# The last product of a fused scan, GLU and ReLU-squared kernel, turned so that the weights stand in the array and 512 tokens move

## The chip, the cores and the metric

One Trainium2 chip, one core of it. The metric is the device time of one execution in microseconds, the median of several runs; lower is better.

## The reference

Three stages follow each other on 3072 tokens of 256 features. The first is a chunked state-space scan over 4 batches and 8 heads, the second a gated feed-forward layer, the third a feed-forward layer with a squared ReLU. Only the third is touched:

```python
def _moe_ref(x, w_gate, w_val, w_out):
    g = x @ w_gate
    silu = g * (1.0 / (1.0 + np.exp(-g)))
    val = x @ w_val
    return (silu * val @ w_out).astype(np.float32)

def _moe2_ref(x, w_in, w_out):          # 256 -> 2048 -> 256
    h = x @ w_in
    r = np.maximum(h, 0.0)
    g = r * r
    return (g @ w_out).astype(np.float32)

def reference(**kwargs):
    attn_out = _attn_ref(**attn_kwargs)          # (4, 8, 768, 32)
    B, H, S, D = attn_out.shape
    x = np.ascontiguousarray(attn_out.transpose(0, 2, 1, 3)).reshape(B * S, H * D)
    x = _moe_ref(x=x, **moe_kwargs)
    return _moe2_ref(x=x, **moe2_kwargs)
```

The output is 3072 rows (tokens) of 256 float32 values, so a row is 1024 bytes.

## The kernel before, in words

**Precision.** A float32 product is made of three products of a reduced float32 type (`F32R`): every operand is split into a high and a low part, and high·high, high·low and low·high are summed in PSUM. So a product of 128 by 128 weights costs three matmuls where plain arithmetic would take one.

**Stages.** The scan works in chunks of 112 tokens, the GLU (`glu`, lines 713 to 827) and the third stage (`relu2`, lines 853 to 934) in tiles of 512 tokens. Activations lie in SBUF with features on partitions and tokens along the row (`xh_all`, `xl_all`: the high and low parts). Their products therefore hold weights in the array and move tokens, and give features on partitions again. The weights arrive by DMA, are converted, and are split into high and low parts (class `Unit`).

**The third stage.** `relu2(i, f, ...)` is called for six token tiles `i` and sixteen blocks `f` of 128 hidden features, 96 calls. Each adds these operations to a graph:

- `front` (line 860, on TensorE): six matmuls that move 512 tokens, 128 hidden features by 512 tokens, into a PSUM bank `h`.
- `relu` (ScalarE, line 870), `square` (VectorE, 873), `high` (ScalarE, 876) and `rest` (VectorE, 880): the squared ReLU, and its split into `p`, high and low.
- `back` (line 882, on TensorE): the last product. Before, tokens stand in the array (128 of `p` at a time, four quarters `q`) and 256 columns of `w_out` move: 4 × 3 = 12 matmuls of 256 columns. They add to two PSUM banks `acc`, each with 2 × 128 tokens on partitions and all 256 output features along the row.
- After the sixteenth `f` the two banks are copied out, one by ScalarE (line 921) and one by VectorE (line 923), and each goes to DRAM in one DMA of 256 KB, whole rows of 1024 bytes (line 927). The sixth tile does this in halves.

**What sets the order.** Every operation has an engine, an estimated cost, a priority, and the buffers it takes from pools: eight PSUM banks (`ps`), four SBUF tiles for `t` and for the copied-out sums `o` (`tmp`), three for `p`. `Graph.order` (lines 50 to 124) replays this graph with the estimated costs and writes out the order in which each engine gets its instructions. A buffer goes to the next operation that asks for its pool, so an operation may wait for whoever used the buffer last: a `relu` that gets a `tmp` tile from which a store reads has to wait for the store to land.

In what follows F20 is the `front` of the 21st call, B20 its `back`; the calls are counted through, from 0 to 95, so that B15 is the last back of the first tile.

Of the kernel before, what the change touches and what calls it, by code (L numbers as in the profile page):

```python
# [8 lines left out]
F32 = mybir.dt.float32  # L9
# [118 lines left out]
def kernel(  # L128
# [13 lines left out]
    nc = tc.nc  # L142
    NB, H, S, D = x.shape
    NS = B.shape[-1]
    T = NB * S
# [5 lines left out]
    NF, NF2 = FF // 128, FF2 // 128  # L151
    P = 128
# [4 lines left out]
    TN = 512  # L157
# [3 lines left out]
    for b in range(NB):  # L161
        t = 0
# [24 lines left out]
    g = Graph(pools)  # L187
# [21 lines left out]
    def new(buf, shape, dtype, tag=None):  # L209
        n = 1  # L210
        for d in shape[1:]:
            n *= d
        if buf.pool in ("L", "ab") and n < 1024:

            t = tp[buf.pool].tile([P, 1024], dtype, tag=buf.pool, name=tag or buf.pool)[:, :n]
            buf.t = t.rearrange("p (a b) -> p a b", a=shape[1]) if len(shape) == 3 else t
        else:
            buf.t = tp[buf.pool].tile(shape, dtype, tag=buf.pool, name=tag or buf.pool)
        if buf.pool == "ps" and fills:


            t = buf.t.rearrange("p a b -> p (a b)") if len(shape) == 3 else buf.t
            t = t[:, : min(n, 256)]
            for _ in range(fills.pop()):
                nc.tensor.matmul(t, idle[:, : shape[0]], idle[:, : t.shape[-1]], start=True, stop=True)  # L225
        return buf.t
# [95 lines left out]
    def dma(eng, n, cost, move, fn, deps=(), prio=0.0, bufs=()):  # L322

        i = g.add(eng, n * cost, fn, deps, prio, bufs, lat=0)
        o = g.add("DMA", move, None, [i], prio, bufs, lat=1700)
        o.issue = i
        return o
# [371 lines left out]
    def product(ps, terms):  # L699
        for i, (l, r) in enumerate(terms):  # L700
            nc.tensor.matmul(ps, l, r, start=(i == 0), stop=(i == len(terms) - 1))  # L701

    acc, seen, fronts, backs = {}, {}, {}, {}
# [7 lines left out]
    GATE, GATE_A = PLAN["gate"]  # L711
# [141 lines left out]
    def relu2(i, f, prio, deps):  # L853
        t0 = i * TN
        d = slice(t0, t0 + TN)
        u = W2[f // 2]
        ph, tb, pb = Buf("ps"), Buf("tmp"), Buf("p")
        late = True

        def front():  # L860
            h = new(ph, [P, TN], F32, "h")
            terms = []
            for k in range(2):
                c = k * 256 + f % 2 * 128
                hi, lo = u.hi.t[:, c : c + 128], u.lo.t[:, c : c + 128]
                terms += [(hi, xh_all[:, k, d]), (hi, xl_all[:, k, d]), (lo, xh_all[:, k, d])]
            product(h, terms)

        def relu():
            nc.scalar.activation(new(tb, [P, TN], F32, "t"), ph.t, AF.Relu)  # L870

        def square():
            nc.vector.tensor_tensor(tb.t, tb.t, tb.t, op=ALU.mult)  # L873

        def high():
            nc.scalar.activation(new(pb, [P, 2, TN], F32R, "p")[:, 0, :], tb.t, AF.Copy)  # L876

        def rest():
            e = nc.vector if late else nc.gpsimd
            e.tensor_tensor(pb.t[:, 1, :], tb.t, pb.t[:, 0, :].bitcast(F32), op=ALU.subtract)  # L880

        def back():
            if f == 0:
                acc[-1 - i] = [new(b, [P, 512], F32, "acc") for b in accbuf[-1 - i]]
            for q in range(4):
                ps = acc[-1 - i][q // 2][:, q % 2 * 256 : q % 2 * 256 + 256]
                tk = slice(q * 128, q * 128 + 128)
                c = 512 + f % 2 * 256
                hi, lo = u.hi.t[:, c : c + 256], u.lo.t[:, c : c + 256]
                for s, (l, r) in enumerate([(0, hi), (0, lo), (1, hi)]):  # L890

                    nc.tensor.matmul(  # L892
                        ps, pb.t[:, l, tk], r,
                        start=(f == 0 and s == 0 and q % 2 == 0), stop=(f == NF2 - 1 and s == 2),
                        skip_group_check=True,
                    )

        if f == 0:
            accbuf[-1 - i] = [Buf("ps") for _ in range(2)]
        ab = accbuf[-1 - i]  # L900

        o1 = g.add("PE", 6 * 232, front, [u.parts, *deps], prio - 10 * PLAN["lead"], [ph, u.hi, u.lo], lat=260)
        o1.keep = lambda: 0 if ab[0].taken else 2
        o = g.add("ACT", 600, relu, [o1], prio - GATE_A, [ph, tb])
        o = g.add("DVE", 690, square, [o], prio - GATE, [tb], port=True)
        o = g.add("ACT", 625, high, [o], prio - GATE_A, [tb, pb])
        o = g.add("DVE", 690, rest, [o], prio - GATE, [tb, pb], port=True)
        bk = g.add("PE", 12 * 120, back, [o], prio, [*ab, pb, u.hi, u.lo], lat=260)
        if f == NF2 - 1:

            cuts = 2 if i == T // TN - 1 else 1
            for m in range(2):
                for c in range(cuts):
                    ob = Buf("tmp")
                    by_act = (m if cuts == 1 else c) == 0
                    w = 512 // cuts

                    def drain(m=m, ob=ob, by_act=by_act, cs=slice(c * w, c * w + w)):
                        ov = new(ob, [P, 512], F32, "o")[:, : w]
                        if by_act:  # L920
                            nc.scalar.activation(ov, acc[-1 - i][m][:, cs], AF.Copy)
                        else:
                            nc.vector.tensor_copy(ov, acc[-1 - i][m][:, cs])

                    def store(ob=ob, by_act=by_act, r0=t0 + m * 256 + c * (w // 2)):
                        q = nc.scalar if by_act and cuts == 2 else nc.sync
                        q.dma_start(
                            out=out[r0 : r0 + w // 2, :].rearrange("(i p) f -> p i f", p=P),
                            in_=ob.t[:, :w].rearrange("p (i f) -> p i f", f=256),
                        )  # L930

                    o = g.add("ACT" if by_act else "DVE", 690 // cuts, drain, [bk], prio - GATE, [ab[m], ob])
                    dma("ACT" if by_act and cuts == 2 else "SP", 1, 480, 700, store, [o], prio, [ob])
        return o1, bk


# [18 lines left out]
    for i, (j, c0, c1, exact) in enumerate(PLAN["cells"]):  # L955
        ti, o = (0, c0 * Q) if c0 < 3 else (1, c0 * Q - cut)
        n = min(c1 * Q, S) - c0 * Q
        for f in (2 * j, 2 * j + 1):
            deps = [ck[k].xf if exact else ck[k].x for k in range(c0, c1)]
# [14 lines left out]
    for s, (tl, f) in enumerate(steps):  # L974
# [8 lines left out]
        deps = fronts[tiles[0]][-1:] + fronts[tiles[1]][-1:] if s == 0 else [step_ops[-1]]  # L983
# [21 lines left out]
    for i in range(T // TN):  # L1005
        deps0 = [o for tl in tiles for o in done_tile[tl] if tl[0] < (i + 1) * TN and tl[1] > i * TN]
        for f in range(NF2):
            prev, _ = relu2(i, f, 30000 + (i * NF2 + f) * 10, [prev, *(deps0 if f == 0 else [])])
# [4 lines left out]
    with tc.manual_schedule():  # L1013
# [13 lines left out]
PLAN = dict(  # L1027
    chunk_at=[3.6, 14.8, 21.8, 0.0, 3.2, 18.0, 18.5],
    unit_at=[4.1, 0, 22.6, 19.4, 20.4, 41.5, 34.2, 27.1, 30.0],
    split_at=[-0.1, -21.6, 22.5, -12.5, -9.6, 27.7, -0.1, -18.9, -33.9],  # L1030
    cells=[
        (5, 3, 7, 0),
        (4, 0, 3, 0),
        (5, 0, 3, 1),
        (3, 3, 7, 1),
# [16 lines left out]
    lead=2.5,  # L1052
# [33 lines left out]
```

## Time and profile before

| what | value |
|---|---|
| median of 3 runs | 663.46 us (663.18 to 665.47) |
| span of the profiled execution | 662.5 us |
| its own time beside the span | not listed apart from the three runs; their median is 1.0 us above the span |
| TensorE busy | 654.8 us, 99% of the span |
| VectorE, ScalarE, GpSimd busy | 415.5, 329.3, 221.9 us |
| granted TensorE clock, mean | 0.999 |
| third stage, first back to last matmul | 396 to 658.5 us |

The busy time of TensorE counts a matmul until its modelled end, so matmuls that follow each other overlap in the table; how fast they follow is read from the chain of work that ended last, which gives the start and the length of every run of equal matmuls. Its start times lie some 0.17 us behind those of the timeline; lengths are the same.

### The profile page before, as it was taken

The numbers are of one execution on the slowest core, as the hardware profiler recorded it, in microseconds if no ns is written. First come the engines' busy times: TensorE is split into PE (matmuls) and PEld (weight loads), VectorE is DVE, ScalarE is ACT, GpSimd is POOL, SyncE is SP. The second block draws the span as 40 slices with busy tenths as digits, with TensorE's granted clock in tenths as the row PEclk, the third lists the DMA queues.
The fourth block names the chain that finished last, engine by engine and source line by source line (L and its number), as shares of the span: only waits on it lengthen the run. The fifth ranks groups of instructions, "written<-read, shape, count | busy, mean of one in ns | idle before, by whom it ended". The sixth has DMA issues, their size and how long they took to land.

```text
span 662.5 us, 10931 instructions
## 1 busy us (share of the span) xinstructions
PE 654.8 (99%) x4297; PEld 560.9 (85%) x4297; DVE 415.5 (63%) x578; ACT 329.3 (50%) x634; POOL 221.9 (34%) x207
## 2 busy tenths in 40 slices
PE   9999999999999999999999999999999999999997
PEld 7888677899877777777788889999999999999996
DVE  7898796667565756677455698454455544544553
ACT  4667444455544444555544584444444444444443
POOL 4005864947555656656564541000000000000000
PEclk9999999999999999999999999999999999999999
DMA  7767447476465456752422220000000100000000
GB/s 176 210 129 153 134 84 145 88 134 123 100 126 94 81 108 113 171 129 50 142 64 63 64 65 0 1 33 1 1 33 0 33 1 1 33 1 0 33 1 33
DMA packets 134819, 48.88 MB, mean 74 GB/s; under 512 B 120304, under 2 KB 123376, under 8 KB 134768
## 3 DMA queue, kind: packets, MB, share of 16 engines
q1 hardware_dynamic: 134480, 47.92, 32.7%
q8 instruction: 34, 0.56, 0.4%
q10 hardware_dynamic: 288, 0.26, 0.1%
q14 instruction: 17, 0.14, 0.1%
HBM read 33.94 MB, written 3.22 MB: 56 GB/s over the span
## 4 chain that ended last, share of the span: by engine, by line
PE 97%; DMA 1%; SPq 0%; ACT 0%; issue 0%; DVE 0%; ACTq 0%
PE acc L892 21%; PE h L701 20%; PE g L701 18%; PE acc L819 16%; PE v L701 13%; PE ys L648 2%; PE ab L552 1%; PE cb L619 1%; DMA raw<-in_moe_w_val_dram 1%; PE ab L225 1%; PE cb L610 1%; PE turn L687 1%; PE g L225 1%; PE cb L225 0%; PE trb L225 0%
## 5 line engine op out<-in xcount | busy, mean ns | idle before, releaser
L892 PE MATMUL acc<-hi,p 128*128 128x256 f32 x768 | 152.1, 282 | 0.0
L892 PEld LDWEIGHTS acc<-hi,p 128*128 128x128 f32 x768 | 125.5, 191 | 3.9
L792 POOL TENSOR_TENSOR p<-t,p 128x512 fp32r<-128x512 f32 (+4 forms) x74 | 98.0, 1326 | 91.4 <-ACT p L787 89.3
L873 DVE TENSOR_TENSOR t<-t 128x512 f32<-128x512 f32 x96 | 69.2, 722 | 66.1 <-ACT t L870 66.0
L892 PE MATMUL acc<-lo,p 128*128 128x256 f32 x384 | 108.6, 283 | 0.0
L880 DVE TENSOR_TENSOR p<-t,p 128x512 fp32r<-128x512 f32 x96 | 67.8, 709 | 57.2 <-ACT p L876 57.2
L870 ACT ACTIVATE t<-h 128x512 f32<-128x512 f32 x96 | 57.5, 599 | 78.6 <-PE h L701 78.3
L768 DVE SCALAR_TENSOR_TENSOR t<-t,g 128x512 f32<-128x512 f32 (+6 forms) x92 | 51.9, 565 | 71.1 <-ACT t L765 71.0
L876 ACT ACTIVATE p<-t 128x512 fp32r<-128x512 f32 x96 | 60.5, 632 | 63.4 <-DVE t L873 59.9
L819 PE MATMUL acc<-p,hi 128*128 128x512 f32 (+4 forms) x296 | 85.7, 372 | 0.0
L892 PEld LDWEIGHTS acc<-lo,p 128*128 128x128 f32 x384 | 73.3, 191 | 3.5
L701 PE MATMUL h<-xh_all,hi 128*128 128x512 f32 x192 | 75.8, 395 | 0.0
L701 PE MATMUL h<-xl_all,hi 128*128 128x512 f32 x192 | 75.8, 395 | 0.0
L701 PE MATMUL h<-xh_all,lo 128*128 128x512 f32 x192 | 74.7, 389 | 0.0
L787 ACT ACTIVATE p<-t 128x512 fp32r<-128x512 f32 (+4 forms) x74 | 42.2, 571 | 62.5 <-DVE t L771 58.9
L765 ACT ACTIVATE t<-g 128x512 f32<-128x512 f32 (+6 forms) x92 | 46.1, 503 | 45.3 <-PE g L701 42.6
L701 PE MATMUL g<-xh_all,hi 128*128 128x512 f32 (+4 forms) x176 | 64.4, 366 | 0.0
L701 PE MATMUL g<-xh_all,lo 128*128 128x512 f32 (+4 forms) x176 | 61.4, 349 | 0.0
L701 PE MATMUL g<-xl_all,hi 128*128 128x512 f32 (+4 forms) x176 | 61.3, 349 | 0.0
L819 PEld LDWEIGHTS acc<-p,hi 128*128 128x128 f32 x296 | 52.1, 188 | 10.3 <-issue 2.9
L771 DVE SCALAR_TENSOR_TENSOR t<-t,v 128x512 f32<-128x512 f32 (+2 forms) x66 | 42.9, 649 | 21.6 <-PE v L701 17.2
L415 POOL TENSOR_TENSOR lo<-v,hi 128x1024 fp32r<-128x1024 f32 x17 | 42.8, 2535 | 32.2 <-ACT hi L410 32.0
(97 smaller groups left out, 1148.6 us busy)
## 6 DMA issues: line engine op xcount, KB each, us to landing
ab<-decay SPq DMA_DIRECT2D x21, 452.0 KB, 4.3
raw<-in_moe_w_out_dram SPq DMA_DIRECT2D x14, 512.0 KB, 5.1
raw<-in_moe_w_in_dram SPq DMA_DIRECT2D x8, 512.0 KB, 4.0
raw<-in_moe_w_gate_dram SPq DMA_DIRECT2D x6, 512.0 KB, 4.0
raw<-in_moe_w_val_dram SPq DMA_DIRECT2D x6, 512.0 KB, 5.1
xa<-in_x_dram SPq DMA_DIRECT2D x24, 112.0 KB, 4.1
out_dram<-o SPq DMA_DIRECT2D x10, 256.0 KB, 2.2
bc<-in_B_dram SPq DMA_DIRECT2D x18, 56.0 KB, 2.5
```

The source lines that it names most:

```text
L415: e.tensor_tensor(self.lo.t, self.v.t, self.hi.t.bitcast(F32), op=ALU.subtract)
L701: nc.tensor.matmul(ps, l, r, start=(i == 0), stop=(i == len(terms) - 1))
L765: nc.scalar.activation(t[:, :n], gg(), AF.Tanh, scale=0.5)
L768: nc.vector.scalar_tensor_tensor(tb.t[:, :n], tb.t[:, :n], 1.0, gg(), op0=ALU.add, op1=ALU.mult)
L771: nc.vector.scalar_tensor_tensor(tb.t[:, :n], tb.t[:, :n], 0.5, vv(), op0=ALU.mult, op1=ALU.mult)
L792: e.tensor_tensor(p[:, 1, :n], tb.t[:, :n], p[:, 0, :n].bitcast(F32), op=ALU.subtract)
L819: nc.tensor.matmul(ps, l, r, start=bank not in done_f, stop=f == NF - 1, skip_group_check=True,)
L870: nc.scalar.activation(new(tb, [P, TN], F32, "t"), ph.t, AF.Relu)
L873: nc.vector.tensor_tensor(tb.t, tb.t, tb.t, op=ALU.mult)
L876: nc.scalar.activation(new(pb, [P, 2, TN], F32R, "p")[:, 0, :], tb.t, AF.Copy)
L880: e.tensor_tensor(pb.t[:, 1, :], tb.t, pb.t[:, 0, :].bitcast(F32), op=ALU.subtract)
L892: nc.tensor.matmul(ps, pb.t[:, l, tk], r, start=(f == 0 and s == 0 and q % 2 == 0), stop=(f == NF2 - 1 and s == 2), skip_group_check=True,)
```

## The change

In the first five of the six token tiles `back` is turned. For each of the two halves `m` of the output features, 128 by 128 weights stand in the array and `p` moves, 512 tokens at once: 2 × 3 = 6 matmuls of 512 columns. `acc` then holds output features on partitions and tokens along the row, which is the wrong way round for the output. So VectorE copies both banks out with `transpose`, which turns every 32 by 32 block within itself: partition 32q + t of the result holds, for each of the 16 groups j of 32 tokens, the 32 features from m·128 + 32q on of token 32j + t. Each half is stored with four DMAs of 64 KB, one for each q, in pieces of 32 features, 128 bytes. The sixth tile is as before. The planner's estimate for a front is lowered from 6 × 232 to 6 × 227 ns, and a turned back is estimated at the same.

```diff
+        turned = i < T // TN - 1
...
         def back():
             if f == 0:
                 acc[-1 - i] = [new(b, [P, 512], F32, "acc") for b in accbuf[-1 - i]]
+            c = 512 + f % 2 * 256
+            if turned:
+                for m in range(2):
+                    w = slice(c + m * 128, c + m * 128 + 128)
+                    for s, (l, r) in enumerate([(u.hi, 0), (u.hi, 1), (u.lo, 0)]):
+                        nc.tensor.matmul(
+                            acc[-1 - i][m], l.t[:, w], pb.t[:, r, :],
+                            start=(f == 0 and s == 0), stop=(f == NF2 - 1 and s == 2),
+                        )
+                return
...
-        o1 = g.add("PE", 6 * 232, front, [u.parts, *deps], prio - 10 * PLAN["lead"], [ph, u.hi, u.lo], lat=260)
+        o1 = g.add("PE", 6 * 227, front, [u.parts, *deps], prio - 10 * PLAN["lead"], [ph, u.hi, u.lo], lat=260)
...
-        bk = g.add("PE", 12 * 120, back, [o], prio, [*ab, pb, u.hi, u.lo], lat=260)
+        bk = g.add("PE", 6 * 227 if turned else 12 * 120, back, [o], prio, [*ab, pb, u.hi, u.lo], lat=260)
         if f == NF2 - 1:
 
-            cuts = 2 if i == T // TN - 1 else 1
+            if turned:
+                for m in range(2):
+                    ob = Buf("tmp")
+
+                    def flip(m=m, ob=ob):
+                        nc.vector.transpose(new(ob, [P, 512], F32, "o"), acc[-1 - i][m])
+
+                    def put(m=m, ob=ob):
+                        for q in range(4):
+                            nc.sync.dma_start(
+                                out=out[t0 : t0 + TN, m * 128 + q * 32 : m * 128 + q * 32 + 32].rearrange(
+                                    "(j t) f -> t j f", t=32
+                                ),
+                                in_=ob.t[q * 32 : q * 32 + 32].rearrange("p (j f) -> p j f", f=32),
+                            )
+
+                    o = g.add("DVE", 690, flip, [bk], prio - GATE, [ab[m], ob])
+                    dma("SP", 4, 480, 1700, put, [o], prio, [ob])
+                return o1, bk
+            cuts = 2
```

How this moves instructions, at three places. First TensorE, in the first tile: one front's second half and one back, before:

```order
L701 MATMUL h<-xh_all,hi 128x512
L701 MATMUL h<-xl_all,hi 128x512
L701 MATMUL h<-xh_all,lo 128x512
L892 MATMUL acc<-hi,p 128x256
L892 MATMUL acc<-lo,p 128x256
L892 MATMUL acc<-hi,p 128x256 x2
L892 MATMUL acc<-lo,p 128x256
L892 MATMUL acc<-hi,p 128x256 x2
L892 MATMUL acc<-lo,p 128x256
L892 MATMUL acc<-hi,p 128x256 x2
L892 MATMUL acc<-lo,p 128x256
L892 MATMUL acc<-hi,p 128x256
```

and the same place now:

```order
L701 MATMUL h<-xh_all,hi 128x512
L701 MATMUL h<-xl_all,hi 128x512
L701 MATMUL h<-xh_all,lo 128x512
L891 MATMUL acc<-p,hi 128x512 x2
L891 MATMUL acc<-p,lo 128x512
L891 MATMUL acc<-p,hi 128x512 x2
L891 MATMUL acc<-p,lo 128x512
```

Twelve matmuls of 256 columns have become six of 512. The order in which fronts and backs follow each other is the same from the first to the last: B0 B1 B2 F6 F7 B3 B4 B5 F8 B6 F9 B7 F10 F11 B8 B9, and from there on one front and one back in turn, each back two calls behind the front.

Second VectorE, at the end of the first tile, where the sums are copied out (`o` is the copy), before:

```order
L873 TENSOR_TENSOR t_4535<-t_4535 128x512 [waits Activation_49]
L923 COPY o_4545<-acc_4163 128x512 [waits PE_49]
L880 TENSOR_TENSOR p_4549<-t_4535,p_4549 128x512 [waits Activation_49]
L873 TENSOR_TENSOR t_4567<-t_4567 128x512 [waits Activation_49]
L880 TENSOR_TENSOR p_4578<-t_4567,p_4578 128x512 [waits Activation_49]
```

and now:

```order
L874 TENSOR_TENSOR t_4439<-t_4439 128x512 [waits Activation_49]
L926 STREAM_TRANSPOSE o_4449<-acc_4162 128x512 [waits PE_49]
L926 STREAM_TRANSPOSE o_4453<-acc_4163 128x512 [waits PE_49]
L881 TENSOR_TENSOR p_4451<-t_4439,p_4451 128x512 [waits Activation_49]
L874 TENSOR_TENSOR t_4467<-t_4467 128x512 [waits Activation_49]
```

VectorE copies out both banks instead of one, between the `square` and the `rest` of F17; ScalarE's copy at line 921 is gone.

Third ScalarE, from the `relu` of F17 on; `DMAHW` semaphores are those of DMAs. Before:

```order
L870 ACTIVATE t_4535<-h_4513 128x512 [waits PE_49]
L921 ACTIVATE o_4547<-acc_4162 128x512 [waits PE_49,Activation_49]
L876 ACTIVATE p_4549<-t_4535 128x512 [waits DVE_49]
L870 ACTIVATE t_4567<-h_4538 128x512 [waits PE_49,Activation_49]
L876 ACTIVATE p_4578<-t_4567 128x512 [waits DVE_49]
L870 ACTIVATE t_4593<-h_4571 128x512 [waits PE_49,Activation_49]
L876 ACTIVATE p_4603<-t_4593 128x512 [waits DVE_49]
L870 ACTIVATE t_4618<-h_4596 128x512 [waits DMAHW5_49,PE_49]
L876 ACTIVATE p_4628<-t_4618 128x512 [waits DVE_49]
L870 ACTIVATE t_4643<-h_4621 128x512 [waits DMAHW6_49,PE_49]
```

and now:

```order
L871 ACTIVATE t_4439<-h_4423 128x512 [waits PE_49]
L877 ACTIVATE p_4451<-t_4439 128x512 [waits DVE_49]
L871 ACTIVATE t_4467<-h_4442 128x512 [waits PE_49,Activation_49]
L877 ACTIVATE p_4482<-t_4467 128x512 [waits DVE_49]
L871 ACTIVATE t_4491<-h_4471 128x512 [waits PE_49,Activation_49]
L877 ACTIVATE p_4501<-t_4491 128x512 [waits DVE_49]
L871 ACTIVATE t_4510<-h_4494 128x512 [waits DMAHW6_49,DMAHW5_49,DMAHW7_49,DMAHW0_49,PE_49]
L877 ACTIVATE p_4520<-t_4510 128x512 [waits DVE_49]
L871 ACTIVATE t_4529<-h_4513 128x512 [waits PE_49,Activation_49]
L877 ACTIVATE p_4539<-t_4529 128x512 [waits DVE_49]
L871 ACTIVATE t_4548<-h_4532 128x512 [waits DMAHW3_49,DMAHW2_49,DMAHW4_49,DMAHW1_49,PE_49]
```

Before, the `relu` of F20 and that of F21 take the `tmp` tiles of the two stores; now the `relu` of F20 waits for the four stores of the first half, and that of F22 for the four of the second.

## Rows read from the trace of the kernel before

**Rows 1.** The page, part 1: busy time of each engine, and the queues' HBM traffic.

```profile
PE 654.8 (99%) x4297; PEld 560.9 (85%) x4297; DVE 415.5 (63%) x578; ACT 329.3 (50%) x634; POOL 221.9 (34%) x207
...
HBM read 33.94 MB, written 3.22 MB: 56 GB/s over the span
```

**Rows 2.** Busy time by stretch: PE, PEld, DVE, ACT, POOL, clock, DMA share, GB/s.

```profile
520.00:560.00 40.00, 40.00 (x257) 36.34 (x256) 20.16 (x30) 18.12 (x30) 0.00 (x0) 1.00 0.04 14
```

**Rows 3.** Who waited for whom: TensorE, the whole span (total, times, longest).

```profile
PE turn L687 <- ACT st L682: 1.3, 1, 1.3
PE ab L225 <- DVE idle L207: 1.1, 1, 1.1
PE ys L648 <- issue: 1.1, 1, 1.1
```

**Rows 4.** Chain that ended last: start us, length us, what; third stage.

```profile
387.94 4.08 PE h L701 x18
392.02 1.36 PE acc L819 x6
393.38 2.72 PE h L701 x12
396.10 4.31 PE acc L892 x36
400.41 2.75 PE h L701 x12
...
407.47 1.39 PE h L701 x6
408.86 1.43 PE acc L892 x12
...
614.70 1.43 PE acc L892 x12
616.13 1.39 PE h L701 x6
```

**Rows 5.** Timeline around the first tile's end: TensorE, ScalarE, VectorE and the store queue.

```profile
434.06 0.28 PE L892 MATMUL acc<-hi,p 128*128 128x256 f32 x1
434.25 0.60 ACT L870 ACTIVATE t<-h 128x512 f32<-128x512 f32 x1 [0.83 <-PE h L701]
434.89 0.69 DVE L873 TENSOR_TENSOR t<-t 128x512 f32<-128x512 f32 x1 [0.74 <-ACT t L870]
435.03 0.60 ACT L921 ACTIVATE o<-acc 128x512 f32<-128x512 f32 x1 [0.17 <-PE acc L892]
435.69 0.69 DVE L923 COPY o<-acc 128x512 f32<-128x512 f32 x1
436.30 0.68 DVE L880 TENSOR_TENSOR p<-t,p 128x512 fp32r<-128x512 f32 x1
...
439.69 0.28 PE L892 MATMUL acc<-hi,p 128*128 128x256 f32 x1
...
439.95 0.60 ACT L870 ACTIVATE t<-h 128x512 f32<-128x512 f32 x1 [0.83 <-PE h L701]
441.97 0.69 DVE L880 TENSOR_TENSOR p<-t,p 128x512 fp32r<-128x512 f32 x1 [0.70 <-ACT p L876]
```

**Rows 6.** VectorE by line: busy us, mean ns of one, idle before.

```profile
L561 DVE TENSOR_TENSOR_SCAN L<-ab,delta 128x452 f32<-128x452 f32 x14 | 14.8, 1087 | 3.9 <-PE ab L552 3.9
L923 DVE COPY o<-acc 128x512 f32<-128x512 f32 x5 | 3.5, 692 | 0.6
```

**Rows 7.** DMA issues: KB each, median us from issue to landing; then `xa` alone.

```profile
xa<-in_x_dram SPq DMA_DIRECT2D x24, 112.0 KB, 4.1
out_dram<-o SPq DMA_DIRECT2D x10, 256.0 KB, 2.2
...
DMA to landing us min/median/max: 2.1/4.0/5.3
```

**Rows 8.** SyncE's timeline: two issues in a row, and one load of `xa`.

```profile
354.65 0.37 SPq L374 DMA_DIRECT2D raw<-in_moe_w_in_dram  x1
355.07 0.47 SPq L374 DMA_DIRECT2D raw<-in_moe_w_out_dram  x1
...
265.67 0.31 SPq L446 DMA_DIRECT2D xa<-in_x_dram  x1
```

**Rows 9.** By stretch, as rows 2: that load of `xa` alone.

```profile
266.60:267.60 1.00, 1.00 (x7) 0.75 (x6) 0.96 (x3) 0.13 (x1) 1.00 (x2) 1.00 0.73 115
```

More of the change, by code (lines that the diff above doesn't have):

```diff
@@ L887, in back @@
                 tk = slice(q * 128, q * 128 + 128)
-                c = 512 + f % 2 * 256
                 hi, lo = u.hi.t[:, c : c + 256], u.lo.t[:, c : c + 256]
@@ L914, in relu2 @@
                     ob = Buf("tmp")
-                    by_act = (m if cuts == 1 else c) == 0
+                    by_act = c == 0
                     w = 512 // cuts
@@ L925, in store @@
                     def store(ob=ob, by_act=by_act, r0=t0 + m * 256 + c * (w // 2)):
-                        q = nc.scalar if by_act and cuts == 2 else nc.sync
+                        q = nc.scalar if by_act else nc.sync
                         q.dma_start(
@@ L932, in relu2 @@
                     o = g.add("ACT" if by_act else "DVE", 690 // cuts, drain, [bk], prio - GATE, [ab[m], ob])
-                    dma("ACT" if by_act and cuts == 2 else "SP", 1, 480, 700, store, [o], prio, [ob])
+                    dma("ACT" if by_act else "SP", 1, 480, 700, store, [o], prio, [ob])
         return o1, bk
```

## The prediction

> **What bounds the kernel now.** The first thing to read is the busy time of the engines: TensorE 99%, VectorE 63%, ScalarE 50% [rows 1]. A busy share is an average, so the next view is a stretch of the third stage by itself: between 520 and 560 us TensorE is busy for all 40.00 us, at a granted clock of 1.00 (2.4 GHz), while VectorE works half of the time, ScalarE 45%, GpSimd not at all and the DMA engines 4% [rows 2]. Then who waited for whom: TensorE's waits of the whole span are three, 1.1 to 1.3 us each, and none of them is for something of the third stage [rows 3]. So this stage lasts as long as TensorE needs for its matmuls, one after the other, and a change in their pace is worth its full length. That pace stands in the chain of waits, which gives runs of equal matmuls with their lengths [rows 4]: a back of twelve matmuls takes 1.43 us between fronts, three backs in a row 4.31 (1.44 each). A front of six takes 1.39 when it follows a back, and 1.36 when it follows another front or anything else that moves 512 tokens (18 matmuls in 4.08, and the second front of the pair in 2.75).
>
> **The twelve matmuls become six.** A 256-column matmul costs 120 ns (1.44 / 12) and a 512-column one 227 ns (1.36 / 6), so two small ones cost 240 where one large one costs 227. The new back is a form that the kernel already runs: the GLU's last product at line 819 holds high and low weights and moves `p`, 512 tokens at a time, and six of those took 1.36 us between two fronts [rows 4]. I take 1.36 for a turned back. The front behind it then follows 512-column matmuls, so I take 1.36 for it too, and not 1.39. In the chain, the first back starts at 396.10 and the 80th (the last one turned) ends at 616.13: 220.03 us, in which lie 80 backs and 76 fronts, F6 to F81. Now they are 156 × 1.36 = 212.16 us, so 7.87 us less; F82 behind them loses the 0.03 as well. Sum: **7.9 us**. The other end of this term is that both keep the slower pace of a front that follows a back, 1.39: 156 × 1.39 = 216.84, a gain of 3.2 us. I take 7.9, because the line 819 row is the nearest in operation, shape and neighbours.
>
> The Trainium skill, page "TensorE: Matmul & The Clock Gate", section "Back-to-back issue gap", gives N / 2.4 + 2.5 ns for a lone warm matmul: 109 ns at 256 columns and 216 at 512. By that the back would go from 1.31 to 1.29 us and the sum would be about 1.2 us. The rows differ from it, with 120 and 227, and they decide; it stands below as a rival.
>
> **The copying out.** ScalarE loses one 0.60 us copy per tile, and VectorE's one copy of 0.69 becomes two transposes [rows 5]. The trace holds no transpose. The plain copy of the same 128 by 512 sums takes 692 ns; the slowest float32 work per element is the scan, 1087 ns for 452 columns, 1.23 us for 512 [rows 6]. I take 0.69, with 1.23 as the upper end. Either is hidden. B15 starts at 434.06, and the square of F17 ends at 435.58; two transposes of 0.69 end at 437.0 and the `rest` of F17 at 437.7, instead of 436.98. B17 uses it: B15, F18, B16 and F19 stand between, 4 × 1.36 = 5.44 us, so its second matmul, the one that reads the low part, is due at 439.7. That leaves 2.0 us, and each transpose could take about 1.65 us before TensorE waits. The PSUM banks are given back 0.7 us later too; the next front that asks for one of them is F22, at about 446.
>
> **The stores.** Two DMAs of 256 KB in pieces of 1024 bytes become eight of 64 KB in pieces of 128, 4096 pieces a tile, all on SyncE, which issues nothing else then. Issues stand 0.42 us apart [rows 8], so the eight are out within 3.4 us, SyncE is free, and nothing is queued behind them. What can wait is the `relu` of F20, for the four stores of the first half, and that of F22, for those of the second; ScalarE works in order, so a late store holds up all that comes behind. By the sequence of pieces F20 ends at 434.06 + 6 × 1.36 = 442.2, its `relu` starts some 0.2 later (0.19 and 0.26 behind the next back's start [rows 5]) at 442.4, and that of F22 at 447.9. There is room beyond that: from the start of a `relu` to the end of its `rest` are 2.71 us (439.95 to 442.66), and the second matmul of the back is due 4 × 1.36 + 0.23 = 5.67 us after the front's end, so a `relu` may come 2.7 us late before TensorE stands.
>
> How long do 4096 pieces of 128 bytes take? Nearest are the loads of `xa`, 112 KB in 896 pieces of 128 bytes (32 floats of a head). They land in 4.0 us at the median and 2.1 at best, against 2.2 for a 256 KB store in long pieces [rows 7]. One that ran alone was issued at 265.67, moved from about 266.60 on, and the DMA engines carried 115 GB/s in that microsecond [rows 8, 9]. At 115 GB/s a tile's 524 KB need 4.6 us; from an issue at 436.4 the bytes would run from 437.3 to 441.9, half of them by 439.6. Both are in time for 442.4 and 447.9, so I take 0. At the other end, all of the 4.0 us counted as moving gives 29 GB/s and 18.3 us, which is too late.
>
> That bound is a load's; these are writes. The Trainium skill speaks against this change here: "DMA: Bandwidth & Descriptors", section "Specifications", says that below 512 bytes the DMA engine reads, modifies and writes. As an estimate from that, double traffic would be 9.2 us a tile, and the sum would stay the same, since the second half has 13 us; HBM reads, 33.94 MB now, would grow by up to 2.6 MB. No run here shows it yet.
>
> **Sum.** Span 662.5 − 7.9 = 654.6. The median of the runs stands 1.0 us above the span of the profiled execution, so **655.6 us**, 1.2% faster. Half a percent, 3.3 us, is about what a measurement of this kernel can tell from no change.
>
> **Rivals.**
>
> *Stores too slow (slower).* The mechanism: short writes hold the two `tmp` tiles, the `relu` of F20 and F22 wait, and the fronts' chain runs dry. It decides once the second half is later than 450.6, that is 524 KB in over 13.3 us, under 39 GB/s, a third of the load's rate. At 29 GB/s each tile loses 18.3 − 13.3 = 5.0 us, five tiles 25: **681 us**. For it speaks that the writes are not in the trace; against it the 115 GB/s and the idle DMA engines of this stage. Chance 0.05.
>
> *Transposes too slow.* Two at four times the copy, 2.77 us each, exceed 1.65 twice: 2.2 us a tile, 11 in all: **667 us**. Against it: nothing that VectorE does here on 512 float32 columns takes half as long. Chance 0.03.
>
> *The turned back keeps the slow pace.* If loading new weights for each product costs what it costs in a front behind a back, the gain is 3.2 us, **660.3 us**. Line 819 speaks against it. Chance 0.04.
>
> *Columns alone set the pace.* If 3072 columns cost the same in six pieces as in twelve, nothing is gained: **663 us**. In that case a back would cost the 1.36 of a front already, and it costs 1.43 [rows 4]. Chance 0.02. By the Trainium skill's formula above it would be 662.
>
> **How the numbers follow.** The forecast has 0.86. Its own spread is small: a few tenths where fronts come in pairs early in the stage and a `rest` is used sooner, and about 1 us of run-to-run spread. Faster by over 0.5% (below 660.1) takes the forecast and a share of the slow pace: 0.89. Within 0.5%: slow pace and columns alone, 0.05. Slower: stores and transposes, 0.06. The range runs from 654.3, the full sum and the lower side of the spread, to 658.5, a third of the gain lost or some half a microsecond of waiting per tile; the rivals lie outside.
>
> **What would show it.** In the chain after: fronts and backs all of 1.36 us up to about 608 us, with backs of 1.43 and fronts of 1.39 only in the sixth tile. Transposes of about 0.7 us, ten of them. Stores landing in 2 to 5 us, and no wait of ScalarE for a DMA. VectorE some 3.5 us busier, ScalarE 3.0 less. The prediction is wrong if the backs take 1.39 or more, or if TensorE shows waits in the first calls of each new tile, five times alike.

## The result and the profile after

The changed kernel took **655.91 us** (median of 4 runs, 655.31 to 657.71) against 663.49 for the kernel before (4 runs, 663.18 to 665.47): a ratio of 0.9881, 95% interval 0.9860 to 0.9901. Run a second time beside the experiments it took 655.99, ratio 0.9882 (0.9868 to 0.9897); two executions of the kernel before that took 1305 us there are left out of that ratio. The forecast was 655.6, from 654.3 to 658.5. The profiled execution took 655.31 us with a span of 653.6.

The page of the changed kernel: busy time of each engine, and HBM traffic.

```profile
PE 646.6 (99%) x3817; PEld 535.9 (82%) x3817; DVE 418.1 (64%) x583; ACT 326.2 (50%) x629; POOL 221.8 (34%) x207
...
HBM read 33.94 MB, written 3.22 MB: 57 GB/s over the span
```

Against [rows 1], TensorE has 480 matmuls fewer (80 backs × 6) and 8.2 us less busy time. VectorE has 2.6 us more, ScalarE 3.1 less. HBM is read exactly as much as before.

The chain that ended last, third stage (start us, length us, what). Lines have moved: the turned back is L891, the old one, now for the sixth tile alone, L902.

```profile
395.19 4.08 PE acc L891 x18
399.27 2.72 PE h L701 x12
...
406.07 1.36 PE h L701 x6
...
607.35 1.36 PE h L701 x6
608.71 1.43 PE acc L902 x12
610.14 1.39 PE h L701 x6
...
645.37 4.32 PE acc L902 x36
```

Where [rows 4] have 1.43 and 1.39, all is 1.36 as far as 608.71, and the old lengths return with the sixth tile. From the first back to the last matmul the stage lasts 645.37 + 4.32 − 395.19 = 254.50 us. In the profile of before the same chain runs from 396.10 [rows 4] to this last row, which is 262.40:

```profile
654.18 4.32 PE acc L892 x36
```

**The stage is 7.90 us shorter.**

TensorE's waits in the whole span (total, times, longest):

```profile
PE turn L687 <- ACT st L682: 1.8, 1, 1.8
PE ab L225 <- DVE idle L207: 1.1, 1, 1.1
```

None lies in the third stage, as in [rows 3]. So neither the transposes nor the stores came onto the path; ScalarE, too, waited for no store anywhere in the trace. The timeline at the end of the first tile, the place of [rows 5], shows where they went:

```profile
432.57 0.69 DVE L874 TENSOR_TENSOR t<-t 128x512 f32<-128x512 f32 x1 [0.64 <-ACT t L871]
433.19 1.31 DVE L926 STREAM_TRANSPOSE o<-acc 128x512 f32<-128x512 f32 x2
433.92 4.21 SPq L930 DMA_DIRECT2D out_dram<-o  x8
434.42 0.65 DVE L881 TENSOR_TENSOR p<-t,p 128x512 fp32r<-128x512 f32 x1
...
437.19 0.61 PE L891 MATMUL acc<-p,hi 128*128 128x512 f32 x2
...
440.11 0.60 ACT L871 ACTIVATE t<-h 128x512 f32<-128x512 f32 x1 [0.67 <-PE h L701]
```

The two transposes of 433.19 take no longer than two copies would (2 × 0.69). The `rest` behind them ends at 435.07; B17 starts at 437.19, and its second matmul, the first that reads the low part, 0.23 later at 437.42. So 2.35 us were left, where 2.0 were forecast. The stores, by stretch (PE, PEld, DVE, ACT, POOL, clock, DMA share, GB/s):

```profile
434.00:436.00 2.00, 2.00 (x10) 1.67 (x9) 1.71 (x3) 0.60 (x1) 0.00 (x0) 1.00 0.42 72
436.00:438.00 2.00, 2.00 (x10) 1.65 (x10) 0.74 (x2) 1.19 (x2) 0.00 (x0) 1.00 0.72 124
438.00:440.00 2.00, 2.00 (x11) 1.65 (x10) 1.23 (x2) 0.68 (x2) 0.00 (x0) 1.00 0.39 66
440.00:442.00 2.00, 2.00 (x11) 1.65 (x10) 0.85 (x2) 1.14 (x2) 0.00 (x0) 1.00 0.00 0
```

(72 + 124 + 66) × 2 us = 524 KB: the whole tile is written by 440.00, before the `relu` of F20 at 440.11 asks for the first half of the buffers. The forty stores by tile (issue ns min/median/max, first and last issue), and the landing of these and of the sixth tile's four:

```profile
L930 SPq DMA_DIRECT2D out_dram<-o x40: 315/510/513, 433.9 to 611.7; - x40
...
DMA to landing us min/median/max: 1.7/1.9/3.7
```

### The profile page after: what moved, and what is told of

Read it like the earlier page. It is cut to its first block, busy times and chain, and to the rows that moved or that the text cites. A ratio compares the mean times of both kernels' runs of the same rounds, so it can differ in the third digit from the quotient of the medians.

```text
span 653.6 us, 10024 instructions
## 1 busy us (share of the span) xinstructions
PE 646.6 (99%) x3817; PEld 535.9 (82%) x3817; DVE 418.1 (64%) x583; ACT 326.2 (50%) x629; POOL 221.8 (34%) x207
## 3 DMA queue, kind: packets, MB, share of 16 engines
HBM read 33.94 MB, written 3.22 MB: 57 GB/s over the span
## 4 chain that ended last, share of the span: by engine, by line
PE 97%; DMA 1%; SPq 0%; ACT 0%; DVE 0%; issue 0%; ACTq 0%
PE h L701 20%; PE g L701 18%; PE acc L891 17%; PE acc L819 16%; PE v L701 13%; PE acc L902 4%; PE ys L648 2%; PE ab L552 1%; PE cb L619 1%; DMA raw<-in_moe_w_val_dram 1%; PE ab L225 1%; PE cb L610 1%; PE turn L687 1%; PE g L225 1%; PE cb L225 0%; PE trb L225 0%
## 5 line engine op out<-in xcount | busy, mean ns | idle before, releaser
L891 PE MATMUL acc<-p,hi 128*128 128x512 f32 x320 | 98.4, 389 | 0.0
L891 PEld LDWEIGHTS acc<-p,hi 128*128 128x128 f32 x320 | 60.1, 188 | 12.4
L891 PE MATMUL acc<-p,lo 128*128 128x512 f32 x160 | 62.2, 389 | 0.0
L819 PEld LDWEIGHTS acc<-p,hi 128*128 128x128 f32 x296 | 52.1, 188 | 10.3 <-issue 2.9
L819 PE MATMUL acc<-p,lo 128*128 128x512 f32 (+4 forms) x148 | 53.4, 361 | 0.0
```

The costliest lines, as they stand in the source:

```text
L819: nc.tensor.matmul(ps, l, r, start=bank not in done_f, stop=f == NF - 1, skip_group_check=True,)
L891: nc.tensor.matmul(acc[-1 - i][m], l.t[:, w], pb.t[:, r, :], start=(f == 0 and s == 0), stop=(f == NF2 - 1 and s == 2),)
```

## The experiments

The theory: only the matmul pace of the backs and fronts moved the time, and the copying out and the stores are covered.

**1. The product alone.** The new product, with the plain copies and whole-row stores of before. The first pair of lines is the condition of the new copying out; left out are lines that give one bank to ScalarE and both stores to SyncE.

```diff
-            if turned:
+            if False:
...
-            cuts = 2
+            cuts = 1 if turned else 2
```

> The turned product alone: the sums are copied out plainly, one bank by ScalarE and one by VectorE, and stored in two DMAs of whole 1024-byte rows per tile, as in the kernel before. It leaves out the turning of the sums, so the output has its values in other places. Theory (the whole gain is TensorE's pace, copying out and storing cost nothing): 655.9 us, as the changed kernel, within 1 us, and backs of 1.36 us in the chain of waits. Rival A (the transposes or the short stores cost something that the pace has to pay for): faster than the changed kernel, 654 or less. Rival B (part of the gain comes from ScalarE's lost copy): slower, 657 or more.

Measured: 655.45 us, ratio 0.9868 (0.9847 to 0.9888). Chain:

```profile
395.15 4.08 PE acc L891 x18
...
645.33 4.32 PE acc L902 x36
```

254.50 us, to the last digit the stage of the whole change. The transposes and 128-byte stores cost nothing that shows.

**2. The copying out alone.** The old product, with the transposes and the 128-byte stores; the condition is the one in `back`, and the planner's estimate of a back is the old one again.

```diff
-            if turned:
+            if False:
```

> The other half of the change alone: backs of twelve 256-column matmuls with tokens standing in the array, as in the kernel before, but both banks turned by VectorE and stored in eight DMAs of 128-byte pieces per tile. The blocks that are turned then hold other values, so the output is not the layer's. Theory: 663.5 us, as the kernel before, within 1 us; backs 1.43 us, fronts behind them 1.39. Rival A (transposes or stores cost): over 664.5. Rival B (ScalarE's lost copy brings part of the gain): under 662.

Measured: 664.31 us (10 runs), ratio 1.0000 (0.9988 to 1.0013). Chain:

```profile
397.01 4.31 PE acc L902 x36
...
655.11 4.32 PE acc L902 x36
```

262.42 us, the stage of before. The two parts together with the whole settle who brought the gain.

**3. Turned, but in halves.** Weights and tokens change places as in the change, but every product is cut into two of 256 columns, on the same weights (the flags behind the operands are left out).

```diff
-    nc.tensor.matmul(acc[-1 - i][m], l.t[:, w], pb.t[:, r, :],
+    for v in (0, 256):
+        nc.tensor.matmul(acc[-1 - i][m][:, v : v + 256], l.t[:, w], pb.t[:, r, v : v + 256],
...
```

> As the changed kernel, but each 512-column matmul of the turned back is cut into two of 256 tokens with the same weights: twelve matmuls of 256 columns again, only with weights standing instead of tokens. Theory (the gain is that of 512 columns per matmul, whichever operand stands): 120 ns each again, backs of 1.43 and fronts behind them of 1.39, so 663.5 us. Rival (it is the turning itself, weights in the array and p moving, that is cheaper, or the same weights twice in a row cost only one load): backs of 1.36 or less and 655.9 us or less.

Measured: 663.47 us (10 runs), ratio 0.9997 (0.9987 to 1.0006). Chain:

```profile
395.40 4.31 PE acc L892 x36
...
422.24 1.43 PE acc L892 x12
423.67 1.39 PE h L701 x6
...
653.48 4.32 PE acc L904 x36
```

262.40 us again, with the 1.39 of the front behind the back. So the gain is that of six matmuls of 512 columns in the place of twelve of 256, and not of which operand is held. The page of this run counts 4297 weight loads beside 4297 matmuls, so every half loaded its weights anew: whether the time goes with the columns per matmul or with the number of weight loads is not separated. Why 256 columns cost 120 ns, over half of 227, and why the front behind them costs 0.03 more was not tried.

**4. All six tiles turned.** The sixth tile would bring another 1.4 us, but its transposes and short stores have nothing to hide behind.

```diff
-        turned = i < T // TN - 1
+        turned = True
```

In the last tile two of the eight stores go out on ScalarE's queue.

> A version meant to be better: the sixth tile is turned too, and in it half of the last bank's four stores are issued by ScalarE's queue instead of SyncE's. Theory: sixteen backs of 1.43 and fronts of 1.39 become 1.36 each, 0.1 x 13 + 0.08 x 3 = 1.5 us less; the end after the last matmul, 4.1 us now (two half copies, then a 128 KB store), becomes 0.26 + 0.65 for the last transpose, 0.6 for two issues and 2 to 3 us for the last short store to land, 3.5 to 4.5 us. So 654.0 to 655.0. Rival (short stores at the end cost more than the pace gives back, which would be the reason to leave the sixth tile): 656.5 or more.

Measured: 656.60 us, ratio 0.9887 (0.9864 to 0.9910): no better than the change. The end of its timeline:

```profile
647.98 1.42 DVE L926 STREAM_TRANSPOSE o<-acc 128x512 f32<-128x512 f32 x2 [0.82 <-PE acc L891]
...
648.24 0.40 PE L891 MATMUL acc<-p,lo 128*128 128x512 f32 x1
648.72 3.17 SPq L931 DMA_DIRECT2D out_dram<-o  x6
```

From the first back (395.52) to the last matmul's end it takes 253.1 us, 1.4 less than the change. But from there to the end of the span (654.8) are 6.2 us, against 653.6 − 649.69 = 3.9 in the changed kernel. The rival held.

**5 and 6. Each bank turned twice, and four times.** This measures how much room the transposes have. The diff is of run 5; run 6 has `range(4)`.

```diff
-    nc.vector.transpose(new(ob, [P, 512], F32, "o"), acc[-1 - i][m])
+    new(ob, [P, 512], F32, "o")
+    for _ in range(2):
+        nc.vector.transpose(ob.t, acc[-1 - i][m])
```

> As the changed kernel, but VectorE turns each bank twice (the same result written twice): four transposes of 0.65 us a tile instead of two. Theory (the first tile's end leaves about 2.0 us before TensorE waits; two more transposes take 1.3): 655.9 us, TensorE without waits. Rival A (VectorE has no room there): five tiles of 1.3 us more, 662.4.

Measured: 656.41 us, ratio 0.9888 (0.9840 to 0.9935), the stage 254.50 once more, and TensorE without a wait in it. Ten more transposes are free.

> As the changed kernel, but VectorE turns each bank four times: eight transposes of 0.65 us a tile. Theory: six more take 3.9 us; in the trace of the changed kernel they would end at 438.4 in the first tile, the rest of F17 at 439.1, and the second matmul of B17 is due at 437.4, so TensorE waits 1.7 us a tile, 8.5 in all: 664.5 us. Rival A (no room at all): five times 3.9, 675.4. Rival B (VectorE is busy only half of the time, so all of it hides): 655.9.

Measured: 672.59 us, ratio 1.0132 (1.0085 to 1.0179), where 664.5 was expected. The stage is 16.4 us longer than the change's. TensorE's waits give 10.1 of it, 2.0 per tile:

```profile
PE acc L891 <- DVE p L881: 8.2, 4, 2.1
PE acc L902 <- DVE p L881: 1.9, 1, 1.9
```

The rest is told by the second of these five places, in the chain and by stretch:

```profile
487.09 2.48 PE h L701 x6
489.57 1.86 PE acc L891 x6
```

```profile
486.00:488.00 2.00, 2.00 (x8) 1.61 (x7) 1.30 (x3) 1.12 (x2) 0.00 (x0) 0.77 0.73 125
488.00:490.00 2.00, 2.00 (x6) 1.52 (x5) 0.90 (x2) 0.96 (x2) 0.00 (x0) 0.50 0.04 9
...
440.00:452.00 12.00, 12.00 (x54) 9.87 (x54) 6.93 (x11) 5.93 (x10) 0.00 (x0) 1.00 0.13 22
```

After the wait the granted clock fell to 0.50 (1.2 GHz), and two groups that take 1.36 took 2.48 and 1.86, 1.6 us more. This happened behind three of the five waits and cost some 4.7 us in all; behind the first wait, as long as the others (last row), it stayed at 1.00. The remaining 1.6 us is some 0.3 us for the first matmuls behind each of the five waits. A wait of TensorE can cost more than it lasts, and the expectation had left that out.

**7 and 8. Stores in pieces of 16 bytes, then with their own buffers.** Eight times the pieces, to bring about the rival of stores too slow; in run 8 the turned sums go to two tiles that the third stage doesn't use, instead of `tmp` (the last pair of lines).

```diff
-    out=out[t0 : t0 + TN, m * 128 + q * 32 : m * 128 + q * 32 + 32].rearrange(
-        "(j t) f -> t j f", t=32
-    ),
-    in_=ob.t[q * 32 : q * 32 + 32].rearrange("p (j f) -> p j f", f=32),
+    out=out[t0 : t0 + TN, :].rearrange("r c -> (r c)").rearrange(
+        "(g t z b) -> t g z b", t=32, z=8, b=4)[:, :, m * 4 + q, :],
+    in_=ob.t[q * 32 : q * 32 + 32].rearrange("p (g b) -> p g b", b=4),
...
-    ob = Buf("tmp")
+    ob = Buf(f"mt{m}")
```

> As the changed kernel, but the stores are cut into pieces of 16 bytes, 32768 a tile instead of 4096, put at other places of the same tile of the output (so the output's values are permuted). Theory (a late store holds the tmp tile that a relu asks for, and TensorE waits once the second half lands over 13.3 us after the first bytes): pieces of 4 to 64 bytes took 8 to 11 ns on an engine, so 2048 pieces on each of 16 take 16 to 20 us, and each of five tiles loses 3 to 7 us: 670 to 690 us, with waits of ScalarE's relu for the DMA, twice a tile at most. Rival (stores are off the path whatever they take, since SyncE and the DMA engines are idle): 655.9.

Measured: 771.23 us, ratio 1.1617 (1.1570 to 1.1665), far beyond the range expected. Third stage of run 7, waits, then ScalarE's timeline, then stretches:

```profile
ACT t L871 <- DMA out_dram<-o: 128.6, 10, 13.6
...
PE acc L891 <- ACT p L877: 70.8, 8, 9.5
...
PE acc L902 <- ACT p L877: 16.5, 2, 8.3
```

```profile
440.80 0.60 ACT L871 ACTIVATE t<-h 128x512 f32<-128x512 f32 x1 [0.73 <-PE h L701]
...
458.99 0.60 ACT L871 ACTIVATE t<-h 128x512 f32<-128x512 f32 x1 [13.47 <-DMA out_dram<-o]
```

```profile
444.00:454.00 10.00, 7.58 (x34) 5.95 (x32) 1.39 (x2) 0.75 (x2) 0.00 (x0) 0.99 1.87 11
454.00:464.00 10.00, 2.98 (x6) 2.11 (x7) 2.99 (x5) 2.83 (x5) 0.00 (x0) 0.50 1.73 12
```

This is the slower rival's mechanism link by link: the `relu` waits for the store of its `tmp`, the `p` comes late, TensorE runs dry (2.98 of 10 us busy) and its clock falls to 0.50 as well. The DMA share stands above 1 there, so it can't be read as a load; the bytes can: at 11 to 12 GB/s a tile's 524 KB take some 46 us. The stage is 115.3 us longer than the change's, of which TensorE's waits give 87.3 (70.8 + 16.5). One thing differs from the change besides the pieces: the buffers come round in another order. The `relu` of F20 (440.80) waits for no store here; those that wait are F22 (458.99) and F26, not F20 and F22.

> As the run with pieces of 16 bytes, but the turned sums are put into two tiles that nothing uses in the third stage, so no relu asks for them. Theory (it is the held tmp tile through which slow stores reach TensorE): 655.9 us, within 1 us, though the stores take as long. Rival (the traffic itself slows the stage, through SBUF or the queue): as slow as with pieces of 16 bytes in the tmp tiles.

Measured: 666.99 us, ratio 1.0035 (1.0013 to 1.0057), where 655.9 was expected. Run 8, stretch and the only wait for a store:

```profile
454.00:464.00 10.00, 10.00 (x46) 8.29 (x45) 5.02 (x8) 4.57 (x8) 0.00 (x0) 1.00 1.70 13
```

```profile
DVE mt L927 <- DMA out_dram<-mt: 7.0, 2, 5.5
```

The stores are as slow (13 GB/s), yet TensorE is full: the shared `tmp` was the link. The number was missed in part because the stores of one tile now outlast a tile's 43.5 us, and the next transposes wait. The stage is 7.6 us longer than the change's: 4.3 are two waits of TensorE, some 2.6 the clock, again 0.50, behind the longer of them (3.2 us), and some 0.7 the first matmuls behind both. The rest lies outside the stage: this execution reached it at 397.84, 2.65 us later than the change (its clock had fallen at 59 us, as in the last section), and the end behind the last matmul is 2.2 us longer.

**9. The changed kernel again** gave the second ratio of the first paragraph.

> The changed kernel once more, beside the next run on the same chip. 655.9 us within 0.7.

**10. Six tiles turned, the last three backs by bank.** An attempt on a faster kernel: as run 4, but the first bank is finished early, so that its transpose and stores run beside the matmuls of the second.

```diff
...
+    late3 = i == T // TN - 1 and f >= NF2 - 3
+    todo = [(0, f, u, pb, c), (1, f, u, pb, c)]
+    if late3:
+        kept3.append((1, f, u, pb, c))
+        todo = todo[:1] + (kept3 if f == NF2 - 1 else [])
+    for m, ff, uu, pp, cc in todo:
...
```

> All six tiles turned, as in the run before with six, but the last three backs first add to the first bank and then to the second, so the first bank is complete 2.04 us before TensorE ends, and its transpose and four stores go out under the last nine matmuls. Theory (the six-tile version lost at the end what its pace gained, because SyncE issued six short stores after the last matmul, 0.53 us apart): the end after the last matmul shrinks from 6.3 us to about 4.2 (0.26 + 0.65 for the transpose, two issues on each of two queues, some 2.5 for 256 KB in short pieces), so 1.5 us less than the changed kernel in the backs and 0.3 more at the end: 654.7 us. Rival (the short stores alone take over 5 us at the end, however they are issued): 656 or more, no faster than the changed kernel.

Measured: 658.67 us, ratio 0.9912 (0.9898 to 0.9927), slower than run 4. The end of its chain:

```profile
647.54 0.64 ACT p L878
...
648.95 2.85 PE acc L897 x11
```

With six matmuls moved behind, the last back reaches its first product too early, and its `p` is not there: the chain leaves TensorE for the last front's `relu`, square, `high` and `rest`. The stage took 254.5 us to the last matmul, which gives back the 1.4 of run 4; the end after it is 0.8 shorter (5.4). So stage and end together are 0.6 us longer than in run 4; of the rest of the difference, 1.75 us in the two traces lie ahead of the stage (397.27 against 395.52), with the clock event of the last section. Neither version with six turned tiles beats the changed kernel.

**11 and 12. Pieces of 32 bytes, shared and own buffers.** As 7 and 8, with `b=8`.

> As the changed kernel, but stores in pieces of 32 bytes, 16384 a tile (the output's values permuted). The run with pieces of 16 bytes moved 11 to 13 GB/s, some 20 ns for a piece on each of 16 engines. Theory (a store's time goes by its number of pieces): 1024 on each engine, 21 us a tile; in the first tile the second half lands at about 456 and the relu of F22 can come at 448.3 at the latest, so 7.7 us a tile are lost, 38 in all, and a few more through a lower clock after each wait: 694 to 710. Rival (the time goes by something else, such as the writes below 64 bytes at 12 GB/s whatever their size): 42 us a tile, as with 16 bytes, 771.

Measured: 653.97 us, ratio 0.9851 (0.9831 to 0.9871), no stall at all, against an expectation of 694 to 710. Run 11 by stretch:

```profile
438.00:440.00 2.00, 2.00 (x10) 1.68 (x9) 0.92 (x2) 1.00 (x2) 0.00 (x0) 1.00 0.93 54
440.00:442.00 2.00, 2.00 (x10) 1.65 (x10) 1.04 (x2) 0.86 (x2) 0.00 (x0) 1.00 1.68 42
...
446.00:448.00 2.00, 2.00 (x11) 1.65 (x10) 1.09 (x2) 0.90 (x2) 0.00 (x0) 1.00 0.00 0
```

The tile is out by 446, at 54 to 42 GB/s, just above the 39 GB/s at which the prediction let the stall begin. But here, too, the waits moved: in the order of instructions they stand before the `relu` of F21 and F23, a call later than in the change, so the change's own waits at this rate were not run. The stage is 254.50 us, so nothing is faster here than in the change.

> As the run with pieces of 32 bytes, but the turned sums lie in two tiles that no relu asks for and that the next tile needs 43 us later, when 21 us of stores have landed. Theory (slow stores reach TensorE only through the tmp tiles that they hold): 655.9 us within 1 us, TensorE at full clock while the stores run. Rival (the traffic slows the stage by itself): over 660.

Measured: 655.57 us, ratio 0.9875 (0.9855 to 0.9895), stage 254.50, as expected. From 32 bytes to 16 the rate falls to about a quarter (54 and 42 GB/s to 11 and 12), where a fixed time per piece would give a half and a fixed rate no fall, and both of the expectations of run 11 fall. How far it falls from 128 bytes to 32 is not known, since the 124 GB/s at 128 are only the pace of the issues (below). Why 16-byte pieces are so much slower stays open.

## Why the prediction was right, point by point

*What bounds.* Right: TensorE is full in the third stage, and a change of its pace was worth its whole length, 7.90 us in the trace against 7.9 forecast.

*Twelve become six.* Right in every length: 1.36 for a turned back, 1.36 for the front behind it. The row of line 819 carried it. Run 3 adds what the row could not: held weights are not the reason, matmuls of 512 columns (with half the weight loads) are. The rival that the back keeps the slow pace (660.3) falls with the chain, and so does the one that columns alone set it (663). The Trainium skill's formula ("TensorE: Matmul & The Clock Gate", section "Back-to-back issue gap"), which stands there for a lone matmul, gave 662; these runs differ from it, as the 120 and 227 ns of before had.

*Copying out.* Right: a transpose of 128 by 512 float32 takes 0.69 us, the same as the copy. VectorE grew by 2.6 us and not 3.5, in part since pairs overlap (1.31 for two). The room was 1.65 per transpose by forecast. Run 5 with two (1.4 per bank) shows no wait, run 6 with four (2.9 per bank) 2.0 us per tile; 2 × (2.9 − 1.65) = 2.5 is what the bound would give, and the 2.35 us of room that the trace showed, for the 2.0 forecast, are most of that difference.

*Stores.* Right that they hide, with two sizes off. Issues stand 0.53 us apart (8 in 4.21 us), not 0.42; the row used was of loads in long pieces. And the rate was 124 GB/s in the full stretch against the load's 115, but neither figure is what 128-byte pieces can do. 64 KB every 0.53 us are 124 GB/s, so the stores went as fast as SyncE issued them, with the DMA engines at 0.72. The 115 is the whole load of 112 KB spread over the microsecond that was read; in the trace of before a quarter of that microsecond shows:

```profile
267.10:267.35 0.25, 0.25 (x4) 0.23 (x3) 0.25 (x2) 0.00 (x0) 0.25 (x2) 1.00 1.14 176
```

The Trainium skill ("DMA: Bandwidth & Descriptors", section "Specifications") speaks of a read, modify and write below 512 bytes. No run shows it: HBM reads stay at 33.94 MB, where by the prediction's estimate it would have added up to 2.6, and by the busy time that the view counts 128-byte writes moved no less than these reads (124 / 0.72 = 172, 176 / 1.14 = 154).

*The slower rival.* Its mechanism is real, as run 7 shows, and its threshold of 39 GB/s lies between a rate that stalls (12) and one that doesn't (42), though both were run with waits at later calls than the change's, so the threshold itself is not shown. Its price was not confirmed: by its sum a tile whose stores take 46 us loses 46 − 13.3 = 32.7 us, and run 7 lost 115.3 / 5 = 23.1, where the relus that wait come later than in that sum. What the sum left out is the lower clock of a starved TensorE: with the first matmuls behind each wait it is 115.3 − 87.3 = 28.0 us of the loss. What spared the change is that 128-byte writes kept up with the issues, at three times the threshold.

*The sum.* Two terms of it were off and nearly cancel, which is luck. The span fell by 8.9 us, not 7.9: this execution reached the third stage at 395.19 and that of before at 396.10. These 0.9 us are already there at 66 us, far ahead of anything that was edited, and the clock stayed at 1.00 in both; they are a difference between executions (below). And the step from span to time is 1.7 to 1.9 us in every execution of this study that lists both, not 1.0: the span of 662.5 belongs to an execution of about 664.2, and was set against a median of 663.46. 654.6 + 1.0 was forecast, 653.6 + 1.7 came.

## What to carry to other kernels

Where TensorE alone is full, count its instructions by shape: find the time per matmul at both widths in the chain, and try turning a product if that puts more columns into each; the price is looked up in a row of the same shape and neighbours. What the turning costs elsewhere is then a matter of due times, not of busy time: ask when each transpose and each store is next waited for, and how much later it may be. A store in short pieces did no harm here while its buffer wasn't asked for, and a wait of TensorE should be priced with the clock that it may lose.

## What was not expected of the hardware

*A part of the spread between runs goes with a clock event.* TensorE waits once early on for ScalarE, 1.3 us in the profile of before [rows 3]. By stretch, first in run 2, then in the changed kernel:

```profile
58.00:62.00 4.00, 4.00 (x20) 3.77 (x20) 3.96 (x4) 3.56 (x7) 2.64 (x2) 0.57 0.50 58
```

```profile
58.00:62.00 4.00, 4.00 (x34) 3.79 (x33) 3.97 (x4) 4.00 (x9) 2.67 (x2) 1.00 0.49 58
```

In both the wait ended near 57.2 and lasted 1.8 us. In the first the clock then fell (0.57, 20 matmuls in the stretch), in the second it did not (34). Run 2 reaches the third stage at 397.01, the change at 395.19. Its ten executions fall in two groups by the mean granted clock: 664.82 to 665.25 us at 0.997, 662.52 to 663.80 at 0.999 or 1.000. The event itself is seen only in executions with a trace (runs 2, 8 and 10); for the others it is inferred from the mean clock. It would be some 1.7 us of a spread of 2.7 in run 2, and it lies far ahead of the edit. It is not all: eleven traces without it reach the third stage anywhere from 394.65 (run 11) to 396.10 us (before), and why is open.

*Short waits can lower the clock, and need not:* three of five waits of 2.0 us did in run 6.

*Short writes:* 124 GB/s or more at 128 bytes (as fast as they were issued), 54 to 42 at 32, 11 to 12 at 16, and with them landing times of 1.9, 4.9 and 15.0 us at the median.
